# Transposing an expert's rows and results on VectorE instead of TensorE in a DeltaNet and hash-routed expert kernel

## The chip, the cores and the metric

The kernel runs on one core of a Trainium2 chip. The metric is the device time of one execution in microseconds. The core has TensorE (PE, with its weight loads as PEld), VectorE (DVE), ScalarE (ACT), GpSimd (POOL) and SyncE (SP); DMAs are issued from the queues of SP, ACT and POOL.

## The reference

Two blocks in a row. The first is a DeltaNet recurrence over 768 steps for 4 x 8 heads of dimension 48; its output y is laid out as x, 3072 rows of 384. The second sends each row to one of eight experts by a hash of its token and applies a two-layer network.

```python
# q, k, v: (4, 8, 768, 48), beta: (4, 8, 768)
for t in range(S):
    kt, vt, bt = (k_n[:, :, t], v[:, :, t], beta[:, :, t, None])
    y[:, :, t] = einsum('bhd,bhde->bhe', q[:, :, t], state)
    v_old = einsum('bhde,bhd->bhe', state, kt)
    state = state + bt[:, :, :, None] * einsum('bhd,bhe->bhde', kt, vt - v_old)
x = y.transpose(0, 2, 1, 3).reshape(3072, 384)

expert_idx = token_ids * 2654435761 % 8      # w1: (8, 384, 1024), w2: (8, 1024, 384)
for e in range(8):
    mask = expert_idx == e
    h = maximum(x[mask] @ w1[e], 0.0)
    out[mask] = h @ w2[e]
```

With the inputs used, the eight experts get 364, 389, 385, 423, 360, 376, 420 and 355 rows. All is float32.

## The kernel before, in words

**Order.** The order of instructions is written out by hand (`tc.manual_schedule()`); each engine runs its own list in that order, and waits where it needs another's result.

**The recurrence** runs over 24 chunks of 32 steps (`NU` chunks, index c), all 32 heads at once in two halves. A chunk is a fixed pattern of small products: `ks` (keys times state, then R = V minus that, on VectorE), `w`, `s` (the state's update), `ys` and `ym` (the output). It needs the inverse of a triangular matrix for each group of four chunks (`invert`), which VectorE works out step by step in the gaps, in portions given in microseconds (`inv.do(5.6)`). `spread_t` and `spread_m` copy that inverse and a masked Gram matrix into block-diagonal tiles (TB by SP, MB by POOL). `store_x` writes a finished chunk's rows to the scratch tensor `x_scratch` in memory, by four DMAs on SP.

**Routing** (`routing()`) is work on VectorE with a few products on TensorE. It is cut into portions in the same way and put into chunks 19 to 22 (`route.do`, `route.products`). From the tokens it works out, for each expert and each of its places, the row to fetch (`gx`) and the row to write (`gidx`), the number of rows of each expert in steps of 16 (`wid_i`), and a list of overflow blocks for experts with more than `CAP` = 424 rows. None overflow here. Its token ids come by four DMAs on SP, issued when `routing()` starts, in chunk 16. The first 318 places (`KE` = 3 tiles of `TS` = 106) of expert 0 are only given to rows of the first `CE` = 21 chunks, so that three gathers can start before the last chunks are done.

**The experts.** For each expert four gathers (`fetch`, `gather`, POOL) bring 4 x 106 rows with rows on partitions. `turn` has TensorE transpose each tile (three 128-column pieces against the identity, into a PSUM bank), and ScalarE or VectorE copies it into xT, features on partitions. `gemm1` is W1 times xT, `relu` takes each of its eight blocks (fo) out of PSUM, ScalarE the even ones and VectorE the odd. `gemm2` is W2 times h, with three blocks (co), copied out into yT. `put` has TensorE transpose yT back, 112 columns at a time, copies that to o_sb, and scatters the rows to the output (POOL).

The matrix products run over as many columns as the expert has rows, rounded up to one of five widths (360, 376, 392, 408, 424): `choose` makes a branch with five arms on TensorE, and `hint` announces the branch ahead of time. Experts 1 to 6 have two such branches, the first four blocks of `gemm1` and all of `gemm2`; the last four blocks of `gemm1` always take 424 columns. `put` of expert e-1 and `turn` of expert e+1 stand within `gemm1` of expert e. Each PSUM bank has its fixed use (`ROWS`, `COLS`). Three sets of weights are kept; `load_w` for e+3 is issued by SP after expert e. In the last expert `gemm2` is cut into columns 0 to 324 and 324 to 424, so that three of its four `put` run before the end. After it, `n_ov` is loaded on all engines and a loop over overflow blocks runs `n_ov` times, here none.

Lines used below: L104 gather, L871 the transposes of `turn`, L887 `gemm1`, L912 `gemm2`, L925 the transposes of `put`, L866 the copies, L929 the scatter, L591 R, L532 and L500 transposes by VectorE in `invert`, L376 to L393 routing's last steps, L563 `spread_t` and `spread_m`, L606 the product of `w`.

Of the kernel before, what the change touches and what calls it, by code (L numbers as in the profile page):

```python
# [19 lines left out]
def kernel(  # L20
# [25 lines left out]

    KT = 4
    KE = 3
    TS = 106
    TD = 112  # L50
    CAP = KT * TS
    CE = 21
# [8 lines left out]
    x_early = x_dram[0:CE * C * B]  # L61
# [7 lines left out]
    gx = keep.tile([P, NHI], I32)  # L69
    ov_i = keep.tile([P, NOV + 1], I32)  # L70
    wid_i = keep.tile([P, E], I32)
# [7 lines left out]
    def load_w(e, eng, i=None, dyn=None):  # L79
# [4 lines left out]
        for co in range(CO):  # L84
            yield
            eng.dma_start(out=W1s[i][:, co], in_=s1[co * P:(co + 1) * P])
# [16 lines left out]
    def gather(src, idx, xg):  # L103
        nc.gpsimd.indirect_dma_start(  # L104
            out=xg[0:TD], out_offset=None, in_=src,
            in_offset=bass.IndirectOffsetOnAxis(ap=idx[0:TD], axis=0),
            bounds_check=src.shape[0] - 1, oob_is_err=False)
# [10 lines left out]
    with ExitStack() as phase1:  # L118
# [101 lines left out]
        def routing():  # L220
# [12 lines left out]
            for b in range(B):  # L233
# [10 lines left out]
            nc.gpsimd.memset(cont[:, :, 0:1], 0.0)  # L244
            iota_f = rt.tile([P, P], F32)
# [51 lines left out]
                            scalar2=float(KE * TS), op0=ALU.mult, op1=ALU.add)  # L297
# [11 lines left out]
            for n in WIDTHS[1:-1]:  # L309
                V.scalar_tensor_tensor(out=wid, in0=used, scalar=float(n), in1=wid, op0=ALU.is_gt,  # L310
                                       op1=ALU.add)
            V.tensor_copy(wid_i, wid)
# [14 lines left out]
                            scalar2=float(E * KT * P - CAP - (KT - 1) * (P - TS)), op0=ALU.mult,  # L327
                            op1=ALU.add)
# [8 lines left out]
            yield 0.65  # L337
            slot = rt.tile([P, NTC], F32)
            V.tensor_reduce(slot, rank.rearrange("p e c -> p c e"), axis=AX.X, op=ALU.add)

            yield 1.0
            col = rt.tile([P, NTC], F32)
            V.tensor_scalar(out=col, in0=slot, scalar1=float(TS), scalar2=None, op0=ALU.is_ge)
            for i in range(2, KT):
                V.scalar_tensor_tensor(out=col, in0=slot, scalar=float(TS * i), in1=col,
                                       op0=ALU.is_ge, op1=ALU.add)
            V.scalar_tensor_tensor(out=slot, in0=col, scalar=float(P - TS), in1=slot,
                                   op0=ALU.mult, op1=ALU.add)
# [32 lines left out]
            for i in range(NTC):  # L381
# [11 lines left out]
            V.scalar_tensor_tensor(out=gx, in0=row, scalar=-1.0, in1=none, op0=ALU.add,  # L393
                                   op1=ALU.add)

            yield 1.2
            row_p = rt.tile([P, 3, NHI], I32)
# [9 lines left out]
            V.tensor_tensor(gidx, row, none, op=ALU.add)  # L407
# [11 lines left out]
            V.tensor_copy(ov_i, ovf)  # L419

# [115 lines left out]
        class Work:  # L536

            def __init__(self, it):
                self.it = it
                self.next = next(it, None)  # L540
                self.owed = 0.0
# [526 lines left out]
```

## Time and profile before

| | |
|---|---|
| median of three runs | 566.92 us (563.47 to 570.17) |
| the profiled execution: its time, its span | 566.48 us, 564.9 us |
| mean granted TensorE clock | 0.938 |
| PE, PEld busy | 516.4 us (91%), 385.8 us (68%) |
| DVE, ACT, POOL busy | 264.9 us (47%), 205.7 us (36%), 255.9 us (45%) |
| recurrence, from the start to the last `ym` | 266.1 us |
| experts, from their first product | 268.08 us on |

The page lists busy time by engine; a table of windows gives the same for stretches of time; a line of the timeline or of a group reads: start, length, engine, line of the kernel, operation, what is written and read, shape, count, and in brackets the idle time before it with what ended it. The chain is followed back from the last instruction to what released each, so what stands on it sets the time. A TensorE product of 32-bit numbers appears as two passes, so eight blocks of three weights are 48 entries.

### The profile page before, as it was taken

To read this page: it belongs to the slowest core of one execution; us is meant where nothing else is said; L and a number is where in the kernel's file an instruction comes from. 1 tells how busy PE (TensorE), PEld (TensorE's weight loads), DVE (VectorE), ACT (ScalarE), POOL (GpSimd) and SP (SyncE) were. 2 spreads that over 40 slices of the span, in tenths; PEclk is the share of its full clock that TensorE was granted. 3 is DMA by queue.
4 is the path that set the end of the run, shared out by engine and by line. 5 is a ranking of instruction groups with operands and counts; after the bars stand their busy time and mean duration, and the time that the engine had idled before them with its cause. 6 is when DMAs were issued, how large, how long until landed. Compare 5 with 4: busy or idle time off the path is not lost.

```text
span 564.9 us, 14221 instructions
## 1 busy us (share of the span) xinstructions
PE 516.4 (91%) x5596; PEld 385.8 (68%) x5596; DVE 264.9 (47%) x707; ACT 205.7 (36%) x448; POOL 255.9 (45%) x409
## 2 busy tenths in 40 slices
PE   8969798889898878988999999999999999999993
PEld 7858788888788777976675656555566565655572
DVE  6899987998989988396310201102011020200200
ACT  5857575887787523353110202102011020200100
POOL 9608676878878785673672320504105020110202
PEclk9659897999999977599999999999999999999998
DMA  6926576888688495574698153631436310010101
GB/s 107 183 56 102 105 144 112 148 133 157 123 153 147 75 177 121 110 167 103 214 364 242 43 158 112 193 119 54 150 115 192 124 44 3 11 34 3 48 0 40
DMA packets 130282, 66.22 MB, mean 117 GB/s; under 512 B 112856, under 2 KB 120114, under 8 KB 130176
## 3 DMA queue, kind: packets, MB, share of 16 engines
q1 hardware_dynamic: 113328, 33.12, 28.3%
q0 software_dynamic: 15328, 28.39, 20.3%
q10 hardware_dynamic: 1520, 3.15, 1.8%
q8 instruction: 85, 1.39, 1.1%
q14 instruction: 21, 0.17, 0.1%
HBM read 49.67 MB, written 10.22 MB: 106 GB/s over the span
## 4 chain that ended last, share of the span: by engine, by line
PE 51%; issue 0%; ACT 0%; DVE 0%; POOL 0%; POOLq 0%
PE psT L912 15%; PE psS L887 9%; PE psS L912 8%; PE psK L887 6%; PE psW L887 6%; PE psG L887 3%; PE psT L871 2%; PE psG L925 1%; PE psY L925 1%; POOL out_dram L929 0%; ACT xT L866 0%; PE psG L629 0%; PE psG L599 0%; DVE o_sb L866 0%; ACT h_sb L900 0%
## 5 line engine op out<-in xcount | busy, mean ns | idle before, releaser
L929 POOL DMA_INDIRECT out_dram<-o_sb,gidx x32 | 30.5, 953 | 203.7 <-DVE o_sb L866 179.1
L912 PE MATMUL psT<-h_sb,w 128*128 128x424 f32 (+5 forms) x288 | 88.8, 466 | 0.0
L912 PEld LDWEIGHTS psT<-h_sb,w 128*128 128x128 f32 x288 | 52.3, 190 | 35.1 <-issue 15.9
L175 POOL DMA_DIRECT2D K<-in_k_dram x96 | 55.6, 585 | 43.1 <-PE psS L618 36.1
L529 DVE TENSOR_TENSOR U<-U,tmp 128x31 f32<-128x31 f32 (+15 forms) x186 | 63.8, 343 | 6.4
L527 DVE TENSOR_TENSOR tmp<-U,Ni 128x31 f32<-128x31 f32 (+15 forms) x186 | 63.4, 341 | 5.3
L563 POOL DMA_DIRECT2D MB<-MT x96 | 55.5, 584 | 4.4 <-PE psG L629 1.3
L181 POOL DMA_DIRECT2D V<-in_v_dram x96 | 55.5, 584 | 3.4 <-DMA V<-in_v_dram 1.8
L887 PE MATMUL psS<-xT,w 128*128 128x424 f32 (+5 forms) x162 | 52.2, 467 | 0.0
L606 PE MATMUL psW<-R,TB 128*64 128x48 f32 x736 | 35.0, 237 | 13.1 <-DVE R L591 6.9
L464 PE MATMUL psG<-sd,w 96*64 96x64 f32 x640 | 30.4, 245 | 17.3 <-ACT sd L443 11.8
L618 PE MATMUL psS<-W,K 128*96 128x96 f32 x368 | 44.1, 267 | 1.2 <-ACT W L612 1.2
L912 PE MATMUL psS<-h_sb,w 128*128 128x424 f32 (+5 forms) x144 | 45.1, 466 | 0.0
L612 ACT ACTIVATE W<-psW 64x192 f32<-64x192 f32 x96 | 31.2, 324 | 36.1 <-PE psW L606 34.7
L451 ACT ACTIVATE w<-psT,own 96x512 f32<-96x512 f32 x66 | 43.2, 689 | 0.4
L887 PEld LDWEIGHTS psS<-xT,w 128*128 128x128 f32 x162 | 29.5, 190 | 19.9 <-issue 10.9
L866 DVE COPY yT<-psT 128x424 f32<-128x424 f32 (+2 forms) x9 | 5.0, 551 | 80.7 <-PE psT L912 80.7
L618 PEld LDWEIGHTS psS<-W,K 128*96 128x96 f32 x368 | 39.2, 179 | 3.0 <-ACT W L612 1.4
L606 PEld LDWEIGHTS psW<-R,TB 128*64 128x64 f32 x736 | 30.0, 151 | 15.7 <-DVE R L591 10.4
L464 PEld LDWEIGHTS psG<-sd,w 96*64 96x64 f32 x640 | 26.0, 156 | 20.9 <-ACT sd L443 14.8
L912 PEld LDWEIGHTS psS<-h_sb,w 128*128 128x128 f32 x144 | 26.2, 190 | 17.8 <-issue 9.1
L887 PE MATMUL psK<-xT,w 128*128 128x424 f32 (+5 forms) x108 | 36.6, 475 | 1.5 <-DVE xT L866 0.7
(203 smaller groups left out, 795.6 us busy)
## 6 DMA issues: line engine op xcount, KB each, us to landing
w<-in_moe_w_dram SPq DMA_DIRECT2D x15, 512.0 KB
w<-in_moe_w_dram SPq DMA_DIRECT2D x20, 384.0 KB
Kd<-in_k_dram SPq DMA_DIRECT2D x24, 192.0 KB
Qd<-in_q_dram SPq DMA_DIRECT2D x24, 192.0 KB
K<-in_k_dram POOLq DMA_DIRECT2D x96, 48.0 KB, 2.9
V<-in_v_dram POOLq DMA_DIRECT2D x96, 48.0 KB, 3.6
x_scratch<-x_sb SPq DMA_DIRECT2D x96, 48.0 KB
TB<-TU SPq DMA_DIRECT2D x96, 32.0 KB
```

Of the source, the lines that this page charges most:

```text
L175: nc.gpsimd.dma_start(out=K4s[c % 3][quarter(i), :, i % 2, :], in_=k_r[i, c * C:(c + 1) * C])
L181: nc.gpsimd.dma_start(out=Vs[c][quarter(i)], in_=v_r[i, c * C:(c + 1) * C])
L451: nc.scalar.activation(to[:, :, :, r], psT, ACT.Copy, scale=own[:, r:r + 1])
L464: nc.tensor.matmul(psG[pair(p), hg, j, ks], lhsT=KT[:, j, hg, p].rearrange("p r s -> p (r s)"), rhs=sd[:, j, ks, 2 * hg + p], start=True, ...
L527: V.tensor_tensor(tmp, U[:, j:j + 1, 0:n].to_broadcast([P, m, n]), Ni[:, j, j + 1:, None].to_broadcast([P, m, n]), op=ALU.mult)
L529: V.tensor_tensor(U[:, j + 1:, 0:n], U[:, j + 1:, 0:n], tmp, op=ALU.add)
L563: eng.dma_start(out=dst[quarter(i), :, i, :], in_=src[quarter(i)])
L606: nc.tensor.matmul(psW[pair(p), i], lhsT=TBs[c % 2][:, HT * h + i, 2 * p:2 * p + 2].rearrange("k r t -> k (r t)"), rhs=Rs[h][:, i], start= ...
L612: nc.scalar.activation(Ws[h][pair(p), :, p], psW[pair(p)], ACT.Copy)
L618: nc.tensor.matmul(psS[h][:, i], lhsT=K4s[c % 3][:, HT * h + i], rhs=Ws[h][:, i], start=(c == 0 and i == 0), stop=True, skip_group_check=True)
L887: nc.tensor.matmul(banks[ROWS[fo]][:, part], lhsT=W1s[i][:, co, fo * P:(fo + 1) * P], rhs=xT[:, co, part], start=(co == 0), stop=(co == CO ...
L912: nc.tensor.matmul(banks[COLS[co]][:, part], lhsT=W2w[i][:, fo, co * P:(co + 1) * P], rhs=h_sb[:, fo, part], start=(fo == 0), stop=(fo == ...
```

## The change

Rows come to the experts, and results leave them, through VectorE's transpose of 32x32 blocks, and TensorE no longer transposes for experts 0 to 6.

- A row of 384 is cut into quarters of 96. In the tile `xq`, partition 32a + j holds quarter a of row j of each group of 32 rows; `rows_in` transposes all of it in one VectorE instruction, so that partition p of xT holds features 3p to 3p+2, and the rows of W1 are loaded in that order (still 4 KB pieces).
- For expert 0, nine early gathers and five late ones (`KE` = 9 of 14 groups of 32 rows, `CE` = 20) fetch quarters straight from memory by indices `x4`. For the others `fetch` brings whole rows as before, and `spread_rows` moves their quarters to the four partition groups by 16 DMAs on SP.
- `rows_out` transposes the three PSUM blocks of `gemm2` by three VectorE instructions into `oq`; 14 scatters of 128 quarters (384 B) by indices `g4` write them. yT, o_sb and the copies remain for the last expert and the overflow loop alone.
- PSUM banks are taken in turn (`take_banks`), so that the results of `gemm2` can wait for VectorE.
- Routing starts in chunk 17; its products run in chunk 19 and the first half of chunk 22. New at its end are two sets of four small products (`by_quarter`) that bring indices to the four partition groups. `spread_t` of chunk 17 is issued ahead of the token loads. The last chunk's rows are stored by SP and ACT, two DMAs each.
- Weights of experts 1 and 2 are loaded by SP rather than POOL. Expert 0's `gemm2` has a branch as well. The last expert's `gemm2` is cut at 256 columns, with two `put` behind the end rather than one.
- The overflow loop stands in one arm of a branch on all five engines, `wid_i[:, E]` being 1 where there is no overflow.

```diff
-    KE = 3
-    TS = 106
-    TD = 112
-    CAP = KT * TS
-    CE = 21
+    KE = 9
+    T = 32
+    QD = DIN // 4
+    CAP = 424
+    NB = -(-CAP // T)
+    CE = 20
...
-            eng.dma_start(out=W1s[i][:, co], in_=s1[co * P:(co + 1) * P])
+            eng.dma_start(out=W1s[i][:, co], in_=s1.rearrange("(p c) f -> c p f", c=CO)[co])
...
+            def by_quarter(idx, n):
+                ps = bank(ps_t, "t")[:, :4 * n].rearrange("p (m k) -> p m k", m=4)
+                for m in range(4):
+                    nc.tensor.matmul(ps[:, m], lhsT=sel[:, m].rearrange("p a j -> p (a j)"),
+                                     rhs=idx[:, 0:n], start=True, stop=True)
+                return ps.rearrange("p m k -> p k m")
+
+            ps = by_quarter(gx_f, KT)
+            yield 0.2
+            V.tensor_scalar(out=x4, in0=ps, scalar1=4.0, scalar2=quarter_f[:, 0:1], op0=ALU.mult,
+                            op1=ALU.add)
...
+        spread_t(NU - 2 * GC + 1)
         w_parts = load_w(0, nc.scalar)
...
-                if c == NU - 3:
-                    route.do(3.0)
-                elif c == NU - 2:
-                    route.do(None)
+                if c >= NU - GC:
+                    route.do(3.5 if c < NU - 2 else None)
...
-                if c >= NU - GC - 1:
-                    route.do(None if c >= NU - 2 else 2.0 if c < NU - GC else 4.0)
+                if c >= NU - 2:
+                    route.do(None)
+                elif c > NU - 2 * GC:
+                    route.do(4.5 if c >= NU - GC else 1.0)
+                if c == NU - GC - 1:
+                    route.do(None)
+                    route.products(1)
...
-                for kt in range(KE):
-                    gather(x_early, gx[:, kt:kt + 1], xg0[kt])
+                for m in range(KE):
+                    gather(x_early, x4.rearrange("p k m -> p (k m)")[:, m:m + 1], xq0[:, m])
+                route.products(4)
+                route.do(None)
...
+        def rows_in(xT, xq, ms):
+            nc.vector.transpose(
+                xT[:, :, T * ms.start:T * ms.stop].rearrange("p c (m j) -> p m c j", j=T),
+                xq[:, ms].rearrange("p m (i c) -> p m c i", c=CO))
+
+        def rows_out(e, ps):
+            oq = m_o.tile([P, NB, QD], F32, name="oq")
+            for co in range(CO):
+                nc.vector.transpose(oq[:, :, co::CO],
+                                    ps[co][:, :CW].rearrange("p (m j) -> p m j", j=T))
+            for m in range(NB):
+                scatter(out_quarters, g4[:, e].rearrange("p k m -> p (k m)")[:, m:m + 1],
+                        oq[:, m])
...
+        def spread_rows(e):
+            xqs[e] = m_xq.tile([P, KT * 4, QD], F32, name="xq")
+            xg = xgs.pop(e)
+            to = xqs[e].rearrange("p (k m) f -> p m k f", m=4)
+            for m in range(4):
+                n = len(range(m, NB, 4))
+                for a in range(4):
+                    nc.sync.dma_start(out=to[T * a:T * a + T, m, :n],
+                                      in_=xg[T * m:T * m + T, :n, QD * a:QD * a + QD])
...
+                if e + 2 < E:
+                    fetch(e + 2)
+                rows_out(e - 1, done.pop(e - 1))
                 gemm1(i, xT, h_sb, arms[e], range(4), f"rows{e}")
                 if e + 1 < E:
+                    hint(e, "cols")
                     arms[e + 1] = arm(e + 1)
...
-            for kt in range(KT):
-                if e > 0:
-                    put_one(e - 1, kt)
-                if e + 1 < E:
-                    turn_one(e + 1, kt)
-            if e > 0:
-                gemm1(i, xT, h_sb, ALL, range(5, FO))
+                gemm1(i, xT, h_sb, ALL, range(4, FO))
             if e + 1 < E:
-                if e == 0:
-                    gemm2(i, h_sb, yTs[0], ALL)
-                else:
-                    gemm2(i, h_sb, yTs[e % 2], arms[e], name=f"cols{e}")
+                rows_in(xTs[(e + 1) % 3], xqs.pop(e + 1), slice(0, NB))
+                done[e] = take_banks(CO)
+                gemm2(i, h_sb, arms[e], done[e], name=f"cols{e}")
                 hint(e + 1, "rows")
...
+            if e > 0 and e + 2 < E:
+                spread_rows(e + 2)
...
+        for n in tc.Switch(over, 2, hint="over"):
+            if n == 0:
+                overflows()
```

## The prediction

> **What bounds the kernel now.** I read the page's busy shares first, then the table of windows cut at the experts' boundaries, then the chain that ended last, and only then the timeline around the hand-over from the recurrence to the experts.
>
> Three of the windows, those of experts 1, 3 and 5 (span of time, its length, busy time and count of each engine, clock, DMA):
>
> ```profile
> core 0: us, PE busy (x) PEld busy (x) DVE busy (x) ACT busy (x) POOL busy (x), PEclk, DMA share, GB/s
> 306.50:341.20 34.70, 34.69 (x120) 20.46 (x120) 5.00 (x9) 4.84 (x10) 7.87 (x8) 1.00 0.40 124
> 376.30:413.10 36.80, 36.79 (x121) 20.61 (x121) 5.00 (x9) 4.83 (x10) 7.83 (x8) 1.00 0.40 124
> 446.10:480.50 34.40, 34.13 (x121) 20.85 (x122) 5.00 (x9) 4.84 (x10) 3.83 (x4) 1.00 0.17 53
> ```
>
> Here TensorE is busy for the whole of each window at full clock, while VectorE and ScalarE work 5 us each of 35 and GpSimd 8. So from 268 us on the time is TensorE's own list of work; what leaves that list is gained, what goes to the other three has some 27 us of cover in each expert. The chain shows which part isn't matrix product, here expert 2's:
>
> ```profile
> 349.29 2.14 PE psG L887 x6
> 351.43 0.33 PE psY L925 x3
> 351.76 0.28 PE psT L871 x3
> 352.03 0.01 issue
> 352.04 0.54 PE psG L925 x3
> 352.58 0.28 PE psT L871 x3
> 352.86 0.33 PE psY L925 x3
> 353.19 0.28 PE psT L871 x3
> 353.46 0.33 PE psG L925 x3
> 353.79 0.27 PE psT L871 x3
> 354.06 2.16 PE psK L887 x6
> ```
>
> From 351.43 to 354.06, 2.63 us, TensorE only transposes: four `put` (L925) and four `turn` (L871). All of it is on the chain.
>
> The hand-over, on POOL and PE:
>
> ```profile
> 258.96 1.09 POOL L104 DMA_INDIRECT xT<-x_scratch,gx  x1 [3.00 <-DVE row_p L398]
> 260.35 1.04 POOL L104 DMA_INDIRECT xT<-x_scratch,gx  x1 [0.30 <-issue]
> 261.69 0.99 POOL L104 DMA_INDIRECT xT<-x_scratch,gx  x1 [0.30 <-issue]
> ...
> 268.08 1.87 PE L887 MATMUL psK<-xT,w 128*128 128x318 f32 x6 [0.51 <-ACT xT L866]
> ```
>
> Three gathers, 1.35 us apart, are in SBUF well before the last chunk ends at 266.1, and the first product starts at 268.08. The fourth gather (272.26) needs the last chunk's rows in memory and is covered by the product.
>
> [...] The trace has such transposes: 1.23 us for 128x1024 read and written densely (L500), 1.99 us with a strided output (L532). [...] sixteen L606 products take 0.64 us at 202, and 1.06 us at 212 after a hole of 2.6 us, and again 1.06 at 232 after one of 2.8 us. [...] The new pieces are 384 B; the trace's own x_scratch pieces are 192 B, and the SP queue's 113328 packets, mostly such, hold 28.3% of 16 engines over 564.9 us, that is 22.6 ns each, so I take small pieces as cheap.
>
> **The change part by part.** Sums are made against the profiled execution, 566.48 us (span 564.9 and 1.6 around it); it lies 0.4 us under the median 566.92, which is nothing.
>
> *Steady experts, 1 to 6.* Their TensorE transposes go: 6 x 2.63 = 15.8 us. What takes their place: VectorE turns 128x1344 in (`rows_in`; by the two rows above 1.6 to 2.6 us) and three 128x448 out (`rows_out`; 3 x 0.54 to 0.87), in place of four copies of L866 and half the evictions, so it stays under 10 us of 32. The evictions of yT by ScalarE go. GpSimd now issues 4 gathers and 14 scatters an expert; at 0.95 to 1.0 us and 0.3 between two (L929, L104) that is 18 x 1.3 = 23.4 us of an expert's 30 to 34, up from 8 x 1.3: the cover holds until one costs 1.75 us. SP issues 16 more moves within SBUF (`spread_rows`) at some 0.63 us (four x_scratch issues take 2.52), 10 us, behind the second weights of the expert before and in front of the next weights, whose first use is over 30 us later. The results of the second product wait in PSUM: three banks of eight, taken in turn. Expert e+1's second half needs them 24 products, 8 us, after `rows_out` can start, and `rows_out` takes 1.6 to 2.6 us. So nothing comes back onto the chain: -15.8. Both branches were there before; expert 0 gets one more.
>
> *Expert 0 and the hand-over.* Its index work is done two chunks sooner, but a step is added, four small products and the scaling that make x4. Order before the gathers: VectorE's last compares (L376, 253.48 to 257.04) held the products of L382; now they are done a chunk sooner, and the 1.0 us of L386 to L393, about 0.9 us for the products and 0.2 for x4 follow the chunk's second R. I place the first gather at 258.0 (258.96 before). Nine at 1.4 us (1.35 for 112 rows, 128 now): the ninth starts at 269.2, lands 3.0 us later (xT<-x_scratch, DMA issues) at 272.2, and `rows_in` of 864 columns takes 1.04 to 1.68, I take 1.4. Products start at 273.7, not 268.08: +5.6. The recurrence ends near 268, for the quarter work also holds back R of the last chunk by some 2 us, but the gathers are later still. TensorE then idles over 5 us and starts at half clock; [...] I take 2.3. The early product narrows from 318 to 288 columns: 13.1 us (268.08 to 281.20) x 30/318 = -1.2. The late one widens from 106 to 136: +0.1, since 106 columns take 0.112 us a product (0.67 for six) and 136 of them by the rate of 424 would take 0.114. TensorE's turns go: 0.97 (281.20 to 282.17) and 1.62 (287.77 to 289.39) = -2.6. The second product runs at expert 0's own width. With 364 rows it takes the 376 arm: by expert 5 (5.05 + 10.11 us at 376) against 17.1 at 424, -1.95. Sum: +2.25. The five late gathers (from 273 on, in by 282) and the first `spread_rows` (done near 302) are needed at 287 and 308.
>
> *Chunks 16 to 21.* Moving `spread_t` ahead of the token loads removes the wait for TB at 205.88 (2.59 us in the trace), but R of that chunk comes at 205.3 anyway: -0.6. Routing put earlier costs VectorE about 1.7 us within the inversion and makes chunks 20 and 21 last 9.3 us each (8.0 us of routing by the code's own budgets, 3.5 and 4.5, and 1.25 of R and V) against 10.6 and 7.1. I count 0, already inside the 258.0, and between -6 and +4 for whether the two slow-clock stretches at 206 and 226 shrink or spread.
>
> *Last expert.* The `put` of expert 6 go: 526.78 to 529.03, -2.25. Its second product, cut at 324 columns, took 535.44 to 555.34, 19.9 us with three puts between. Now 48 of 256 columns at 0.215 and 48 of 168 at 0.141 (0.356 at 424, scaled) are 17.1, and two puts 1.0: -1.8. Two scatters follow the last product, not one: +1.25. The loop's semaphores and branches, 560.2 to 561.8, are in an arm not taken: -1.6. Bounds for this end -3 and +3. Sum of this part: -4.4.
>
> Total: -15.8 + 2.25 - 4.4 = -17.95, so 566.48 - 17.95 = 548.5 us.
>
> **The rivals.**
>
> *The slow clock goes.* If the moved `spread_t` keeps the clock up at 206 to 218, ten such microseconds at half rate give back up to 6 us; for it, only a 2.6 us hole stands ahead; against it, R is nearly as late. 542.5 us.
>
> *The hand-over costs more.* Gathers of 1.6 us each, or x4 two microseconds late by the VectorE queue, start the first product at 280, with the expert 1 rows late too (covered by only 6 us): +7. 555.5 us. For it: nine transfers in a row on one queue with nothing behind them. It does not undo the experts' gain.
>
> *Scatters pace the experts.* On POOL, 18 indirect transfers an expert; in the built order each waits for the one eight before it, and each scatter writes 128 pieces of 384 B. If one comes to 2.1 us with its gap, an expert lasts 37.8 us, not 32.4, since oq's two buffers hold back VectorE, its relus and TensorE. Six experts: +32, 580.5 us. It decides from 1.75 us on and is slower than before from about 1.95. For it: [...] 4.5 times as many pieces. Against: 0.95 us for 112 pieces at 2.7 us to landing, with eight in flight at 1.3 us apart.
>
> *The change doesn't do what it says.* TensorE could still transpose; in the built order of the changed kernel experts 1 to 6 have no transposes on PE, so I give it nothing.
>
> **How the numbers follow.** Forecast 0.56, slow clock gone 0.15, dearer hand-over 0.18, scatters 0.11. A change within 1% is what a measurement of this kernel can't tell from none. Faster by more than 1% (under 561.2) is all of the first two and most of the third, 0.83; within 1%, the rest of the third and a mild form of the fourth, 0.07; slower 0.10. The range leaves out the scatters and the ends of the others: 540 to 560.
>
> **What would show it.** Windows of experts 1 to 6 at 31 to 34 us with PE busy throughout, no PE transposes in them, VectorE at 6 to 9 us, POOL at 18 or more: right. A hole of about 5 us ahead of the first product and a PEclk below 1 there: the hand-over's step. The first x4 gather far from 258, or gathers not 1.4 apart, shift expert 0 by as much. Experts longer than 34.5 us with PE waiting on DVE for h_sb or xT, and DVE on scatters, would make the prediction wrong.

## The result, and the profile after

| | before | changed |
|---|---|---|
| time, median of four runs | 568.54 us | 610.50 us (608.66 to 616.52) |
| ratio | | 1.077 (1.065 to 1.088) |
| profiled execution, span | 566.48, 564.9 us | 608.66, 607.0 us |

The forecast was 548.5 us. Later, on another chip, the same changed kernel took 564.23 us against 561.78, ratio 1.006 (1.002 to 1.010). The larger part of the error therefore lies in something that was not there every time, and what remains without it is still no gain. Both are looked at below. A ratio always compares a kernel with the kernel before on the same chip; in all the runs fell on at least six chips, so a few us between experiments on different chips mean nothing. A time is the median of all runs, while a ratio, with its 95% interval, uses only runs within 1.5% of the fastest of their kernel.

The windows of experts 1, 3 and 5 in the changed kernel (stretch, length, busy time and count of PE, PEld, DVE, ACT and POOL, clock, DMA share, GB/s):

```profile
core 0: us, PE busy (x) PEld busy (x) DVE busy (x) ACT busy (x) POOL busy (x), PEclk, DMA share, GB/s
315.90:357.20 41.30, 34.88 (x97) 21.26 (x97) 6.70 (x8) 2.09 (x4) 18.30 (x19) 0.96 0.78 261
398.50:443.10 44.60, 37.56 (x98) 21.74 (x98) 6.70 (x8) 2.09 (x4) 17.86 (x18) 0.89 0.40 122
484.00:518.00 34.00, 31.91 (x96) 21.11 (x97) 6.31 (x8) 2.09 (x4) 13.79 (x14) 1.00 0.26 74
```

TensorE no longer transposes, but it is no longer busy throughout: 6.4 us are missing in the first row and 7.0 in the second, and the clock falls behind the holes, to 0.96 and 0.89. The timeline of expert 1 shows what it waits for:

```profile
326.06 2.30 PE L925 MATMUL psG<-xT,w 128*128 128x424 f32 x6
...
330.32 2.30 PE L925 MATMUL psT<-xT,w 128*128 128x424 f32 x6
...
332.92 3.60 PE L947 MATMUL psT<-h_sb,w 128*128 128x392 f32 x10 [0.29 <-issue]
...
337.80 1.00 POOL L112 DMA_INDIRECT xg<-x_scratch,gx  x1 [0.30 <-issue]
...
340.24 0.60 DVE L940 TENSOR_SCALAR h_sb<-psG 128x424 f32<-128x424 f32 x1 [15.44 <-remote]
...
340.89 4.04 PE L947 MATMUL psT<-h_sb,w 128*128 128x392 f32 x6 [4.38 <-issue]
341.88 0.52 ACT L938 ACTIVATE h_sb<-psY 128x424 f32<-128x424 f32 x1 [13.45 <-remote]
342.01 0.60 DVE L940 TENSOR_SCALAR h_sb<-psT 128x424 f32<-128x424 f32 x1 [1.18 <-remote]
```

The product in psG ends at 328.4. VectorE has nothing else to do, yet its relu starts at 340.24. The ones of psY and psT are 11.4 and 9.4 us late. The second product (L947) needs these relus from its eleventh entry on and stops at 336.5 for 4.38 us. "Remote" means that the update which released it is on record, but no instruction that ended near it. The trace records updates of semaphores, the counters for which an engine waits. For TensorE's semaphore it has none from 322.1 to 340.2, and then nine within 0.35 us from 341.86, which is as many as TensorE owed from the product in psY on. (The records are not complete: two relus, at 324.19 and 327.91, ran within that stretch.) So the products are done, and the news of them is held up (below, the hold-up). It comes 1.4 and 3.1 us after the last of 18 indirect transfers has ended on GpSimd (337.80 + 1.00): 14 scatters and the 4 gathers for a later expert, one each 1.3 us since 315.7. Expert 5 has 14; the last ends at 502.6, the relus come from 505.2 on. In experts 1 to 7 a relu is within 0.6 us of its product if that ends before the ninth transfer of the series starts; behind the tenth nearly all are late, by up to 13.2 us, in expert 6 only the last (3.1 us).

At the hand-over, nine gathers do the same to the recurrence:

```profile
258.91 1.60 PE L651 MATMUL psS<-W,K 128*96 128x96 f32 x8
...
264.19 1.00 POOL L112 DMA_INDIRECT xT<-x_scratch,x  x1 [0.30 <-issue]
...
264.96 0.47 PE L662 MATMUL psG<-W,MB 128*64 128x48 f32 x5 [0.95 <-issue]
...
266.43 0.49 ACT L657 ACTIVATE S<-psS 96x384 f32<-96x384 f32 x1 [10.87 <-remote]
```

ScalarE takes the new state 5.9 us after its product, 1.2 us after the last gather. TensorE itself comes in small groups with holes of near 1 us, at 264.96 for one. That it could put out no more updates would fit, but is not shown.

### The profile page after: what moved, and what is told of

Read it like the earlier page. It is cut to its first block, busy times and chain, and to the rows that moved or that the text cites. A ratio compares the mean times of both kernels' runs of the same rounds, so it can differ in the third digit from the quotient of the medians.

```text
span 607.0 us, 14169 instructions
## 1 busy us (share of the span) xinstructions
PE 514.0 (85%) x5432; PEld 400.8 (66%) x5432; DVE 278.1 (46%) x701; ACT 185.7 (31%) x405; POOL 326.8 (54%) x479
## 4 chain that ended last, share of the span: by engine, by line
issue 28%; PE 25%; DVE 18%; POOL 9%; SPq 7%; another core or an unknown queue 4%; ACT 3%; DMA 3%; POOLq 0%; DVEq 0%; ACTq 0%
POOL out_dram L968 7%; DVE tmp L556 6%; DVE U L558 6%; SPq L1005 5%; PE psW L639 3%; PE psS L651 2%; PE psG L493 2%; PE psT L462 2%; DMA TB<-TU 2%; PE psS L947 2%; PE psK L621 2%; POOL xg L112 1%; PE psT L947 1%; PE psY L662 1%
## 5 line engine op out<-in xcount | busy, mean ns | idle before, releaser
L968 POOL DMA_INDIRECT out_dram<-oq,g x98 | 96.5, 985 | 143.0 <-DVE oq L961 94.0
L639 PE MATMUL psW<-R,TB 128*64 128x48 f32 x736 | 34.8, 235 | 12.8 <-DVE R L624 9.0
L947 PE MATMUL psS<-h_sb,w 128*128 128x392 f32 (+4 forms) x128 | 37.1, 447 | 7.0 <-DVE h_sb L940 7.0
L947 PE MATMUL psT<-h_sb,w 128*128 128x424 f32 (+2 forms) x96 | 37.3, 545 | 4.7 <-issue 4.7
L639 PEld LDWEIGHTS psW<-R,TB 128*64 128x64 f32 x736 | 29.9, 149 | 15.5 <-DVE R L624 12.6
L112 POOL DMA_INDIRECT xg<-x_scratch,gx x28 | 28.2, 1007 | 20.7 <-DMA w<-in_moe_w_dram 12.5
L925 PE MATMUL psT<-xT,w 128*128 128x424 f32 (+4 forms) x108 | 37.2, 496 | 2.1 <-DMA xq<-xg 1.4
L947 PEld LDWEIGHTS psS<-h_sb,w 128*128 128x128 f32 x128 | 29.3, 260 | 14.4 <-DVE h_sb L940 8.1
L947 PEld LDWEIGHTS psT<-h_sb,w 128*128 128x128 f32 x96 | 24.6, 260 | 17.5 <-issue 8.8
L925 PE MATMUL psS<-xT,w 128*128 128x424 f32 (+5 forms) x108 | 34.0, 463 | 2.1 <-DMA w<-in_moe_w_dram 1.7
L657 ACT ACTIVATE S<-psS 96x384 f32<-96x384 f32 x46 | 22.4, 486 | 36.5 <-PE psS L651 25.2
```

Source lines behind the costliest of these rows:

```text
L639: nc.tensor.matmul(psW[pair(p), i], lhsT=TBs[c % 2][:, HT * h + i, 2 * p:2 * p + 2].rearrange("k r t -> k (r t)"), rhs=Rs[h][:, i], start= ...
L925: nc.tensor.matmul(ps[fo][:, part], lhsT=W1s[i][:, co, fo * P:(fo + 1) * P], rhs=xT[:, co, part], start=(co == 0), stop=(co == CO - 1))
L947: nc.tensor.matmul(ps[co][:, part], lhsT=W2w[i][:, fo, co::CO], rhs=h_sb[:, fo, part], start=(fo == 0), stop=(fo == FO - 1))
L968: scat = nc.gpsimd.indirect_dma_start(out=dst, out_offset=bass.IndirectOffsetOnAxis(ap=idx, axis=0), in_=o_sb, in_offset=None, bounds_chec ...
```

## The experiments

Theory A: a dense series of indirect transfers on GpSimd holds up the semaphore updates of the other engines. A1 counts the transfers, A2 their pieces. B: the branches, or the PSUM banks taken in turn. C: full DMA engines. D: a busy GpSimd.

**Four scatters of fourteen; seven and seven.** The first leaves out ten scatters of each expert, the second puts a wait between two groups of seven:

```
-            for m in range(NB):                  # first kernel
+            for m in range(4):
...
+                send(0, 7)                       # second kernel, in rows_out
...
                 gemm1(i, xT, h_sb, ALL, range(4, FO))
+                nc.gpsimd.tensor_copy(pause, h_sb[:, FO - 1, 0:1])
+                send(7, NB)
```

> The changed kernel, but of the 14 scatters of each of experts 0 to 6 only the first 4 are issued, so most of these experts' output is left out. Everything else stays: banks in turn, branches, transposes by VectorE, moves by SP, the 4 gathers. Theory A (a back-to-back series of 14 scatters and 4 gathers on GpSimd holds up the semaphore updates by which VectorE and ScalarE learn of TensorE's products, until about 2.7 us after the last of them): the series is 8 long, the stalls inside the second products of experts 1 to 5 and 7 (4.4, 5.4, 7.0, 7.1, 1.6 and 2.6 us, 28 in sum) go, the second relus run within 1 us of their product; 582 us (576 to 588). Theory B (the branches and hints, or the PSUM banks taken in turn, make the relus late): nothing changes there, 607 to 612 us. Theory C (weights and moves between tiles fill the DMA engines): the scatters are 13 MB less in small pieces but the weights stay, 600 to 610 us.

> The changed kernel with the same 14 scatters an expert, cut in two: 7 behind rows_out, then a one-column GpSimd copy that reads the last relu of the expert (so GpSimd has to stop until that relu is done), then the other 7 and the gathers. Counts, bytes and all other work stay. Theory A: no more than 7 transfers lie ahead of the second relus, these run on time, the stalls inside the second products go; the second 7 and the 4 gathers fall into the second product, which needs no semaphore of VectorE any more; 582 us (576 to 592; more if rows_in or rows_out of the next expert are caught by the second series). Theory B (branches, banks): no change, 607 to 612 us. Theory C (DMA filled): no change, 605 to 612 us.

Measured: 565.53 us, ratio 0.997 (0.994 to 1.000), and 573.17 us (four runs, 567.58 to 582.42), against 567.62 before. Both are below what the sum of the stalls gave. The slow clock behind the stalls goes too: in experts 1 to 4 the changed kernel's trace has 27 us at half clock, that of the first kernel none; and the first has a shorter end, of which more below. (The ten scatters left out in each of seven experts hold 3.4 MB, not 13.) The second keeps every transfer and every byte, and so speaks against B and C. Its timeline:

```profile
323.03 0.97 POOL L972 DMA_INDIRECT out_dram<-oq,g  x1 [0.30 <-issue]
...
330.58 0.60 DVE L940 TENSOR_SCALAR h_sb<-psT 128x424 f32<-128x424 f32 x1 [3.67 <-PE psT L925]
331.34 0.18 POOL L1092 COPY pause<-h_sb 128x1 f32<-128x1 f32 x1 [7.34 <-DVE h_sb L940]
332.10 0.99 POOL L972 DMA_INDIRECT out_dram<-oq,g  x1 [0.57 <-issue]
```

All relus of experts 1 to 7 are within 1.0 us of their product. With four scatters, so eight transfers in a row, three still come 1.2 to 2.6 us late. Nor is the hold-up gone in the second kernel: behind the eleven transfers of a second group `rows_out` starts up to 4.4 us late.

The chip is not the reason. On it the changed kernel without the arm, in the next runs, takes 608.84 us, and in the very executions with four scatters and with seven and seven the thirteen gathers of the hand-over, which were left in a row, make relus 5.0 and 4.2 us late.

**The series put into the kernel before; the arm taken out.**

```
+        def series(n):                           # kernel before, at the start of experts 1 to 7
+            for m in range(n):
+                nc.gpsimd.indirect_dma_start(out=more[:, m], in_=x_quarters, ...)
...
-        for n in tc.Switch(over, 2, hint="over"):   # changed kernel
-            if n == 0:
-                overflows()
+        overflows()
```

> The kernel before, and at the start of each of experts 1 to 7 ten more indirect gathers of 128 pieces of 384 B into a tile that nobody reads; TensorE's transposes, the fixed banks and the four whole-row scatters stay. Theory A: the series on GpSimd grows from 4 to 14, the relus and evictions behind the ninth or tenth are late, stalls of 3 to 7 us in each of six or seven experts: 590 to 610 us. Theory B and C: GpSimd has the time (18 x 1.3 = 23.4 us of 35 per expert) and TensorE sees nothing of it: 566 to 572 us.

> The changed kernel with the overflow loop behind the last expert without a branch around it, as in the kernel before; the branch of five engines and its hint are gone. If the arm makes the longer tail (15.2 us from the last product to the end, 9.6 before): 603 to 606 us. If the tail is longer because two scatters follow the last product and wait for the stalled last expert: no change or +1.6 us, 609 to 613 us.

Measured: 598.89 us, ratio 1.054 (1.047 to 1.061), and 608.84 us. Taking the arm out gains nothing that shows. Of the 33.3 us that the kernel before with the series has more in its span, 13.0 lie in experts 1 to 6, 10.5 in expert 0, which the first series still meets, and 7.6 from expert 7 on, of which 5.9 are a longer drain (an instruction of GpSimd behind all work). With its own banks and branches it gets the hold-up too. Here this catches the evictions of the second product and then TensorE:

```profile
462.52 0.99 POOL L104 DMA_INDIRECT xg<-x_scratch,gx  x1 [0.31 <-issue]
462.67 0.46 PE L913 MATMUL psT<-h_sb,w 128*128 128x360 f32 x1 [0.96 <-issue]
464.07 0.64 PE L913 MATMUL psT<-h_sb,w 128*128 128x360 f32 x1 [0.94 <-issue]
...
466.21 0.51 ACT L867 COPY yT<-psS 128x424 f32<-128x424 f32 x1 [19.41 <-remote]
```

Again the eviction, the copy of a result out of PSUM, is there 2.7 us after the last transfer (462.52 + 0.99). It is 13.0 us late.

**Width and size of the pieces.** Half the partitions, a quarter of them, and whole rows in place of quarters in the series put into the kernel before:

```
-                scatter(out_quarters, g4[:, e]..., oq[:, m])
+                scatter(out_quarters, g4[:64, e]..., oq[:64, m])     # and [:32]
...
-                    out=more[:, m], in_=x_quarters, ...
+                    out=more[:, m], in_=x_dram, ...                  # 1536 B pieces
```

> The changed kernel with all 14 scatters an expert, back to back as before, but each of only the first 64 partitions, so half of the output of experts 0 to 6 is left out. The number of transfers in a series stays 18, the pieces go from 2304 to 1408. Theory A2 ([...] at 128 each 1.29 us, and the ninth or tenth transfer, some 1200 pieces, is where the semaphore updates of the other engines stop): half the rate of pieces, no or short stalls, 568 to 580 us. Theory A1 (the number of transfers): the stalls stay, 600 to 612 us.

> The changed kernel with the 14 scatters an expert of only the first 32 partitions each, so three quarters of the output of experts 0 to 6 are left out. Between the 64 pieces that still stalled (614.8 us) and the 16 of the gathers that did not. If the number of back-to-back transfers decides and each of 32 pieces counts: 600 to 614 us. If a transfer has to be of some width to count: 565 to 580 us.

> The kernel before with ten more gathers of whole rows (128 pieces of 1536 B) at the start of each of experts 1 to 7, in place of ten of 384 B pieces, which made it 31 us longer. If small pieces were what hurts: under 575 us. If it is the number of pieces in a row, of whatever size (theory A2): 590 to 605 us, with four times the bytes adding little, since the queue of weights leaves most of the 35 us free.

Measured: 614.76 us, ratio 1.073 (1.062 to 1.085); 620.04 us (four runs, 613.69 to 624.91, on a chip where the kernel before takes 570.89); and 598.01 us, ratio 1.052 (1.044 to 1.059). So neither the number of pieces, between 32 and 128 a transfer, nor their size takes the hold-up away; A2 falls. The narrower scatters are issued a little faster, one each 1.2 us, and relus are up to 15.5 us late. What builds up, if anything does, is not shown: in the changed kernel's trace GpSimd's queue has 224 packets of 4 B for expert 5's 14 scatters, 16 a scatter, but no run tells whether these matter.

**Pause and rate.**

```
             for m in range(NB):
+                if m == 7:                                # first kernel
+                    for _ in range(4): nc.gpsimd.memset(pause_128x1024, 0.0)
+                if m > 0: nc.gpsimd.memset(pause_128x640, 0.0)    # second kernel
                 scatter(out_quarters, ...)
```

> The changed kernel with four GpSimd memsets of 128x1024 (0.97 us each in the trace, 3.9 us) between the seventh and the eighth scatter of each expert; they wait for nothing of TensorE. If what matters is that the series is broken for longer than the 2.7 us that the relus needed after its end: the second relus, which fall into the first transfers of the second series, run on time, and the time is as with the cut that waits for the relu, 573 us (568 to 580). If the cut helped only because it made GpSimd wait for the relu itself: the stalls stay, 598 to 612 us.

> The changed kernel with a GpSimd memset of 128x640 (about 0.6 us) between any two scatters of an expert: a transfer each 1.9 us in place of 1.29, 14 in a row all the same. If the rate matters (GpSimd gives out transfers faster than something behind it clears them, which frees itself in 2.7 us for some ten): all relus on time, 568 to 580 us. If the number since the last longer pause matters: relus behind the ninth transfer are late; as the ninth now comes 17 us and not 11 us after the first, the stalls are fewer, but rows_out of the next expert is caught; 580 to 600 us.

Measured: 578.32 us, ratio 1.009 (0.991 to 1.027), and 577.67 us, ratio 1.011 (1.007 to 1.015), on the chip of the 32-piece scatters. The timeline of those 32-piece scatters, in expert 1's series (the two relus of psS belong to the two halves of the first line):

```profile
328.50 4.27 PE L925 MATMUL psS<-xT,w 128*128 128x392 f32 x12
...
342.12 1.00 POOL L112 DMA_INDIRECT xg<-x_scratch,gx  x1 [0.30 <-issue]
345.34 0.60 DVE L940 TENSOR_SCALAR h_sb<-psS 128x424 f32<-128x424 f32 x1 [17.95 <-issue]
345.99 1.68 PE L947 MATMUL psT<-h_sb,w 128*128 128x392 f32 x2 [3.86 <-DVE h_sb L940]
347.45 0.53 ACT L938 ACTIVATE h_sb<-psS 128x424 f32<-128x424 f32 x1 [17.19 <-remote]
```

And that of the spaced ones, at the same place of the work:

```profile
331.21 0.98 POOL L971 DMA_INDIRECT out_dram<-oq,g  x1 [0.17 <-issue]
...
332.19 0.65 POOL L966 MEMSET pause<- 128x640 f32 x1
333.00 0.98 POOL L971 DMA_INDIRECT out_dram<-oq,g  x1 [0.17 <-issue]
...
333.29 0.52 ACT L939 ACTIVATE h_sb<-psY 128x424 f32<-128x424 f32 x1 [3.75 <-PE psY L926]
...
335.43 0.60 DVE L941 TENSOR_SCALAR h_sb<-psT 128x424 f32<-128x424 f32 x1 [3.67 <-PE psT L926]
335.56 5.57 PE L948 MATMUL psT<-h_sb,w 128*128 128x392 f32 x16 [0.17 <-issue]
```

With a scatter each 1.8 us no relu of experts 1 to 7 is late, and no `rows_out` behind the scatters either, although in one place 32 transfers follow each other without a longer pause and GpSimd is busier than in any run that was late (385.4 us), which also speaks against D. In the same execution the thirteen gathers of the hand-over, still one each 1.3 us, make relus up to 3.1 us late. So it is the rate: one each 1.2 to 1.3 us for more than some seven or eight is too fast, 1.8 us is not. A pause of 4 us that waits for nothing does as well as the wait for the relu: the relus are on time, and `rows_out` behind the second group of eleven is up to 3.8 us late.

**What the chip has to do with it.** Three attempts at the width and at D:

```
-                    out=more[:, m], ... ap=gx[:, 0:1]             # series in the kernel before
+                    out=more[:16, m], ... ap=gx[:16, 0:1]         # 16 pieces
+                nc.gpsimd.memset(more_128x1344, 0.0)              # memsets in its place
...
-                scatter(out_quarters, g4[:, e]..., oq[:, m])      # changed kernel
+                scatter(out_quarters, g4[:16, e]..., oq[:16, m])
```

> The kernel before with ten more indirect gathers at the start of each of experts 1 to 7, as in the run with 598.9 us, but each of only 16 pieces of 384 B where that had 128. Theory A1 (it is the number of indirect transfers in one series that holds up the semaphore updates): about the same as with 128 pieces, 590 to 600 us. Theory A2 (it is the number of pieces[...]): an eighth of the pieces, 566 to 573 us, and GpSimd's 128-piece gathers behind them leave no trace on TensorE.

> The kernel before with ten GpSimd memsets of 128x1344 at the start of each of experts 1 to 7 in place of the ten more gathers: by 0.97 us for 128x1024 in this trace about 1.27 us each, so GpSimd is as busy as with the gathers and moves nothing by DMA. Theory A (the transfers do it): 566 to 572 us, VectorE and ScalarE on time. Theory D (a busy GpSimd does it, [...]because its later gathers and scatters come 13 us later): 580 to 600 us.

> The changed kernel with the 14 scatters an expert of only the first 16 partitions each, so seven eighths of the output of experts 0 to 6 are left out. Scatters of 128, 64 and 32 pieces, back to back, all stalled TensorE (610.5, 614.8 and 620.0 us); ten gathers of 16 pieces did not. If it is the 16 pieces that made those harmless: no late relus, 565 to 578 us. If it was that they were gathers, or that they stood ahead of the wide ones: the stalls stay, 600 to 622 us.

Measured: 573.31 us, ratio 1.020 (1.014 to 1.027); 571.42 us, ratio 1.018 (1.013 to 1.024); 560.17 us, ratio 0.993 (0.990 to 0.997). They seemed to say that 16 pieces are harmless. But in the last of them the hand-over, which has 128 pieces as ever, showed no late relu either behind 13 transfers in a row, where other chips had delays of up to 3 to 6 us. So the changed kernel itself was run again, with the 16-piece scatters beside it:

> The changed kernel itself, beside the next two on one chip. So far two of five chips, those on which the kernel before took 561 and 562 us, showed no late relu at all, not even behind the thirteen 128-piece gathers of the hand-over, which are the same instructions that made relus 1 to 6 us late on the others (568 to 571 us before). If the hold-up is there on every chip: 605 to 615 us. If it hangs on the chip, and this is one without: 552 to 570 us.

> The changed kernel with scatters of 16 pieces again (seven eighths of the output of experts 0 to 6 left out), now with the changed kernel itself beside it. If narrow transfers are harmless: 555 to 572 us, also where the changed kernel takes over 600. If the first run was on time only because of its chip: as the changed kernel, over 600 us where that stalls.

Measured: 564.23 us, ratio 1.006 (1.002 to 1.010), and 562.37 us, ratio 1.002 (0.999 to 1.005). The changed kernel on this chip, in expert 1:

```profile
321.85 2.30 PE L925 MATMUL psG<-xT,w 128*128 128x424 f32 x6
...
324.19 0.60 DVE L940 TENSOR_SCALAR h_sb<-psG 128x424 f32<-128x424 f32 x1 [3.60 <-PE psG L925]
...
325.29 0.98 POOL L968 DMA_INDIRECT out_dram<-oq,g  x1 [0.30 <-issue]
...
328.31 5.57 PE L947 MATMUL psT<-h_sb,w 128*128 128x392 f32 x16
328.46 0.60 DVE L940 TENSOR_SCALAR h_sb<-psT 128x424 f32<-128x424 f32 x1 [3.67 <-PE psT L925]
```

The program and the 1.29 us are the same; at 325.29 its fourteenth scatter goes out, and the relus start as their products end. The hold-up hangs on the chip, or on something else that lasts through a sitting, since, as far as the record names them, no chip was used a second time. Where the kernel before takes 568 to 571 us it was there, where it takes 561 to 562 us it was not; whether that difference has the same cause wasn't tried. What 16 pieces do on a chip with the hold-up stays open, and so does the test of D by memsets. These two also show that not all of the 31 us of the series need be hold-up: on a chip without it they cost 12.0 and 10.1 us with no late relu, of which the traces name only a part (with 16 pieces the drain takes 5.4 us in place of 2.1).

**Whole rows.** The quarters that VectorE turns out of PSUM are put together within SBUF and leave in four scatters; in the second kernel expert 0's rows also come whole and are turned by TensorE, so that x4 and g4 are not needed. In the third ten gathers into a spare tile were added:

```
-            for m in range(NB):
-                scatter(out_quarters, g4..., oq[:, m])
+            for m in range(4):
+                for a in range(4):
+                    nc.sync.dma_start(out=og[T * m:T * m + T, :n, QD * a:QD * a + QD],
+                                      in_=fr[T * a:T * a + T, m, :n])
+            for kt in range(KT):
+                scatter(out, gidx[:n, e * KT + kt:e * KT + kt + 1], og[:n, kt])
...
-                for m in range(KE): gather(x_early, x4..., xq0[:, m])          # second kernel
+                for kt in range(KE // 4): gather(x_early, gx[:, kt:kt + 1], xg0[kt])
...
+                if e in (3, 5):                                               # third kernel
+                    for m in range(5): gather(..., gx[:, 0:1], more[...])             # a spare tile
```

> The changed kernel, but the quarters that VectorE turns out of PSUM are put together to whole rows within SBUF by 16 moves of SP (spread_rows the other way round), and go out in 4 whole-row scatters of 1536 B pieces, as in the kernel before. The output is whole. Hand-over to expert 0, with its nine quarter gathers, and the arm stay. Theory A: no series longer than 8, the stalls inside the second products go as with four scatters (565.5 us), and the tail from the last product to the end shrinks from 15.2 to about 9 us; 564 us (558 to 570). Rival: SP has 32 moves and 7 weights an expert, some 25 us of 32, and becomes the pacer: rows and weights of the next experts late, 570 to 590 us.

> The one with whole-row results, and the hand-over to expert 0 by whole rows too: two gathers of 128 rows and TensorE's transposes for 256 early columns, two gathers for the other 168, as the kernel before did with three and one; no x4 and g4, so two groups of four small products and their scalings are gone from the routing. The output is whole. Theory A: no nine gathers during the last chunk, which ends at 266 as before; first product near 268, expert 0 lasts 34 us (before 38.2, by the 376 arm and fewer turns), experts 1 to 6 33 us each, last 36.4, tail 9: 548 us (543 to 555). If the hand-over's cost lies elsewhere (loads of experts 1 and 2 behind the moves): within 4 us of the whole-row results alone.

> Whole rows on both sides (552.6 us), and five more gathers of 128 pieces each into a spare tile in experts 3 and 5, which makes 74 indirect transfers, as many as in the kernel with whole-row results alone. There the last GpSimd drain took 1.5 us, here without the ten it took 7.6 us. If the drain hangs on how many transfers or pieces GpSimd has issued in all [...]: 1.5 to 2.1 us again and 546 to 548 us. If it hangs on the end of the program itself (the stretch from the last product on, alike in both): 7.6 us again and 552 to 554 us.

> The version with whole rows on both sides and ten more gathers, once more: 0.965 to 0.98 of the kernel before on whatever chip, 546 to 556 us, since its series stay at 8 or 9 in the experts that matter.

Measured: 557.41 us, ratio 0.987 (0.984 to 0.991); 552.61 us, 0.985 (0.979 to 0.991); 553.32 us, 0.971 (0.962 to 0.980), on a chip with the hold-up; again, on one without, 550.62 us, 0.980 (0.973 to 0.987). The first two ran on a chip without it. So in these four measurements whole rows gain 1 to 3%, with the hold-up or without. SP with 32 moves an expert is no pacer. On the chip with the hold-up five gathers more make a row of thirteen in experts 3 and 5, not of 8 or 9 as the last expectation has it; relus there are up to 8.5 us late, but these experts take 34.2 and 32.0 us, since the last late relu still comes before the second product starts (expert 3: 389.7 and 391.3). Expert 0, behind ten gathers in a row, takes 40.8 us there and 36.8 us on the other chip. The first product of the second kernel starts at 261.5, in the first at 270.0, but most of that is given back at the end, where GpSimd's last drain differs. The drain's line in the second kernel and in the third, here its second run (line, queue, count, shortest, median and longest in ns, first and last start):

```profile
L1117 POOLq DRAIN  x3: 46/104/7581, 541.5 to 549.6; - x3
```

```profile
L1122 POOLq DRAIN  x3: 46/104/1537, 554.8 to 556.9; - x3
```

Ten idle gathers in the middle of the program shorten its end by 6 us. So the code around the drain does not decide its length; it depends on what GpSimd has issued before. By which rule stays open: it took 1.5 to 1.7 us with 74 indirect transfers, 2.1 us with the 64 of the kernel before, 7.6 us with the 64 of the second kernel here, and 7.4 us with the 144 of the changed one, on either kind of chip. The pieces count in it: with the same 144 it took 5.8 us where a scatter had 64 pieces, and 4.2 where it had 32 or 16.

## Why the prediction was wrong

The prediction's steps against the changed kernel's two profiled executions, in us of their spans:

| | before | predicted | changed | changed, chip without hold-up |
|---|---|---|---|---|
| first product at | 268.1 | 273.7 | 273.1 | 270.4 |
| expert 0 | 38.2 | 34.9 | 42.8 | 39.9 |
| experts 1 to 6 | 210.9 | 195.1 | 236.3 | 200.0 |
| expert 7 and tail | 47.7 | 43.3 | 54.8 | 51.8 |
| span | 564.9 | 547.0 | 607.0 | 562.1 |

*Experts 1 to 6.* "So nothing comes back onto the chain: -15.8" is the step that failed, by 41 us. Most prices were right: `rows_in` took 1.99 us, `rows_out` 0.76 to 0.80 us a bank, scatters 0.98 us with 0.30 between, the branches nothing that shows. Only the moves were too cheap: the 16 of an expert took SP 11.3 to 18.8 us from first to last, not 10. An expert without stalls is what was forecast: expert 6 took 34.2 us, 36.8 before, and on the other chip experts 3 to 6 took 2.5 to 2.7 us less each than in the profile of before. The other chip's windows of experts 5 and 6:

```profile
444.80:476.20 31.40, 31.40 (x97) 21.18 (x98) 6.75 (x8) 2.10 (x4) 13.84 (x14) 1.00 0.28 81
476.20:510.30 34.10, 34.10 (x97) 21.14 (x96) 6.73 (x8) 2.10 (x4) 13.78 (x14) 1.00 0.07 20
```

The fault lies in the cover, "18 x 1.3 = 23.4 us of an expert's 30 to 34 ... the cover holds until one costs 1.75 us". It took the time that GpSimd shows for a transfer as all that a transfer takes from the machine. But the 0.98 us of expert 5's last scatter end at 502.6, and packets of its queue run until 503.4. The kernel before has no more than eight in a row, and from eight nothing follows for eighteen. The relus did not wait for GpSimd's time but for updates held up by its rate, and a transfer each 1.8 us, slower than my limit, was the cure. That a dense row holds up updates was not in the prediction at all, nor could the trace of before show it, in which no relu is more than 0.2 us late.

On the chip without the hold-up 5 us are still missing in this row. Expert 1 starts at half clock after 3.0 us without work, and expert 2 lasts as long as before (34.8 us), with a wait of 2.0 us at its end; with whole rows on both sides they took 32.9 and 32.2. That is most of it. The early moves, weights or gathers, which I thought covered, seem to be late; which of them it is the traces don't settle, since they name a gather for the first wait and nothing for the second.

*Hand-over and expert 0.* First product at 273.7 forecast, 273.1 measured, but by another road. The gathers began at 253.5 and not at 258.0, 1.34 us apart and not 1.4, and their rows were there before the chunk ended; the recurrence, forecast to end near 268, ended at 272.5 (268.6 on the other chip), held up as shown above. Two errors cancelled, so that number was luck. TensorE did not idle over 5 us ahead of the first product but 0.6 us (1.8 on the other chip); it starts at half clock all the same, since the slow stretch began within the last chunk, at 255.5, and ran to 276.0. The 2.3 us priced for that were the author's estimate. In the trace of before one such stretch runs from 204.8, within a hole of 2.6 us, to 218.5; what sets its length no run tells. Expert 0 then lost 4.31 us to `rows_in` of the late columns, behind a relu that was 3.0 us late, and 1.4 us to moves for expert 1. Without hold-up it is still 5 us longer than forecast, 3.0 of them the wait ahead of expert 1. The nine gathers, named as a rival ("nine transfers in a row on one queue with nothing behind them"), are the place, but that rival had 7 us for it and the time at 555.5.

*Last expert.* -4.4 forecast, +7.1 measured, +4.1 on the other chip. The last expert up to its last product is 2.4 us shorter on that chip, as the puts and the cut should make it. "Loop -1.6" and the two scatters were beside the point, for what follows TensorE's last instruction takes 15.2 us against 8.9, of which the drain has 7.4 against 2.1. The drain was not priced.

*The rival "Scatters pace the experts"* had the right culprit and came nearest (580.5 us), but was still 30 us short and rests on a mechanism that isn't there: transfers stayed at 1.29 us, and no wait for oq's buffers decides. (An expert's scatters write 14 x 128 = 1792 pieces against 4 x 112 = 448 before, four times as many and not 4.5.) The sign to look for, "PE waiting on DVE for h_sb", came true; "and DVE on scatters" did not. *The rival "The slow clock goes"* did not come true: between 200 us and the first product the clock record has 27 us at half clock before, 38 in the changed kernel and 29 on the other chip. Chunks 16 to 21 were priced at 0; no run here separates them.

## What to carry to other kernels

A transfer that hides in an engine's idle time can still cost the others (relus of the changed kernel came up to 13.2 us late): count how many come in a row and how fast, and compare with the longest such row that the trace already shows (here eighteen against eight). If the new row is longer, spread it (at one each 1.8 us no relu was late) or leave a few us in its middle (with 4 us the ratio was 1.009, without 1.077), or put small pieces together within SBUF and send few large ones (0.971 to 0.987). When a relu or a copy starts long after its product with no releaser named, look for what all late ones have in common in time, and measure the doubtful kernel and its cure side by side on one chip: what looks like a cure may only be another chip.

## What was not expected of the hardware

- Indirect transfers from GpSimd at one each 1.2 to 1.3 us held up semaphore updates of TensorE, from the seventh to the tenth on. Behind 14 to 18 transfers in a row most came 2.6 to 3.5 us after the last with 128 pieces, up to 4.6 us after it with 32. Relus were up to 15.9 us late (the run without the arm), 13.2 in the changed kernel's first trace. At 1.8 us each there was no delay. Pieces of 384 or 1536 B, 32, 64 or 128 a transfer, did not take it away.
- Some chips did this and others, with the same program, didn't: 1.077 and 1.006 for one change. Whether it is the chip or the sitting, what in it, and where the updates wait, no run here tells. Every run on record comes with a span and a clock from the profiler, so none shows the hold-up without one.
- The last drain of GpSimd took 1.5 to 2.1 us in some kernels and 4.2 to 8.0 us in others, and with ten more idle gathers it took 1.5 us in place of 7.6.
